# Placing the start-up work of a fused RWKV6 and tanh-shrink kernel: even loads over the first block's steps, and spaced transfers in the boot

## The chip, the cores and the metric

The kernel runs on one core of one Trainium2 chip. The metric is the time of one execution on the device in microseconds (us); medians and ranges of several executions are given. A profile is one execution, and its span (first to last instruction) is about 2 us shorter than the time. The *granted clock* is the share of full speed that TensorE's throttle allowed; 0.50 is half rate. "E", "first rest", "turn" and "block 1" below are points in a profile, in us from the start of its span.

## The reference

Four batches, eight heads, 768 tokens, 48 channels a head. A linear recurrence with decay w gives y, then a dense layer of 2048 features follows, whose activation is h - tanh(h):

```python
for t in range(S):
    cur = np.einsum('bhd,bhe->bhde', u[None] * kt, vt)
    y[:, :, t] = np.einsum('bhd,bhde->bhe', rt, state + cur)
    state = wt[:, :, :, None] * state + np.einsum('bhd,bhe->bhde', kt, vt)
...
x = y.transpose(0, 2, 1, 3).reshape(B * S, H * D)     # 3072 x 384
h = x @ w_in                                          # 384 x 2048, float64 in
out = (h - np.tanh(h)) @ w_out                        # 2048 x 384
```

## The kernel before

The 3072 tokens are cut into 8 blocks of 384. The recurrence of a block runs as *phases*: scores within chunks of 64 tokens in *levels* 1, 2, 4, 8, 16, 32 (each a batch of small products on TensorE, then decays of `kq` and `rp` and a masked copy on VectorE), a *turn* (transposes of `kq`), an *update* of the states, and a *result* that leaves x transposed in `xT`. A head of 48 channels stands in a slot of 64 rows, and `xT`, 3 x 128 rows, has six such slots. The two heads left over, called `late`, are moved into the six 16-row *holes* of the slots by six small transfers.

The dense layer of a block runs in 16 *steps*, one for each 128 features: `hp` (three products into PSUM, six matmul records), ScalarE reads it and forms squares and tanh, VectorE does five operations (the "rest"), and an accumulation `acc` follows three steps later. The phases of block i + 1 are hung between the steps of block i, so that TensorE stays full. Block 0 has no block before it: all of its phases run in a *boot*, alone. The float64 weights are loaded as pairs of words (`raw`), and *converted* by two operations on ScalarE and three on VectorE for each of 16 parts; six are converted in the boot, ten during block 0.

```python
def convert(f, raw):
    ...
    up = conv.tile([P, 2 * DM], I32, name="up", tag="up", bufs=2)
    nc.scalar.activation(out=a..., in_=hi..., func=AF.Copy, scale=HIGH_SCALE)   # w_sb
    nc.scalar.activation(out=up, in_=lo..., func=AF.Copy, scale=2.0 ** -29)
    return [shift left (VectorE), and/or with hi (VectorE), add up (VectorE)]
...
def start(self, ps):                                   # the boot
    ...
    for m in (2, 4, 8, 16, 32):
        for p0 in HALVES:
            self.level(ps, m, p0, UP)
            self.totals(m, p0, UP)
    for p0 in HALVES:
        self.turn(ps, p0)
        self.update(ps, p0)
    for p0 in HALVES:
        self.result(ps, list(range(p0, p0 + UP)), p0 != HALVES[0])
        if p0 == HALVES[0]:
            self.fill_holes([nc.sync])
...
def plan(i):                                           # which phase at which step
    names = ("level 1", 2, 4, 8, 16, 32, "turn", "update")
    first_step = 3 if i == 0 else 0
    phases = {first_step + n: name for n, name in enumerate(names)}
    result = first_step + len(names) + 1
    ...
    if i == 0:
        put(0, 1, "kmix", "rmix"); put(1, 1, "totals 1", "kq"); put(2, 1, "totals 2", "rp")
    ...                                                # later blocks: in the last six steps
...
for f in range(NF):                                    # the steps of block i
    g, next_rest = first(here, f, ps_d)
    for n, op in enumerate(rest):                      # "rest" of the step before,
        op()
        if n >= 2 and extra:                           # with a conversion woven in
            extra.pop(0)()
    ...
    if later and f in phases:
        later.phase(ps_a, phases[f])
    extra = convert(*raws.pop(0)) if raws else []      # one conversion a step from step 0
    ...
```

So in block 0 the ten conversions come one a step in steps 0 to 9, and block 1's phases come one a step from step 3 on, whatever that adds up to. In the later blocks the phases fill steps 0 to 7 and 9.

## Time and profile before

| before | |
|---|---|
| time, 3 executions | 691.12 us (689.88 to 691.14) |
| span of the profile, mean granted TensorE clock | 688.1 us, 0.984 |
| TensorE / VectorE / ScalarE busy | 94% / 82% / 69% of the span |
| last decay of the boot's levels ends on VectorE ("E") | 31.7 us |
| first `rest` starts on VectorE | 56.46 us |
| turn of block 1 starts on TensorE | 112.23 us |
| block 1's first `hp` starts | 143.94 us |
| from there to the end | 544.2 us |

The timeline of TensorE (start, duration, engine, line, operation, tile, count, and in brackets the idle time before it and who ended it), at the turn and at the start of block 1:

```profile
112.23 1.53 PE L317 MATMUL att<-ident,kq 128*128 128x128 f32 x12 [1.17 <-DVE kq L267]
...
143.94 2.10 PE L476 MATMUL hp<-xT,w_sb 128*128 128x384 f32 x6
```

A block starts at its first `hp`. The turn waits 1.17 us for a decay, a sign that VectorE sets the pace up to there. And the table of transfers between 10 and 40 us (tile, issuing queue, count, size, median us from issue to landing):

```profile
rmix<-in_rT SPq DMA_DIRECT2D x1, 768.0 KB, 8.7
```

A load for block 1, issued at 11.85 us, takes 8.7 us in a queue of others.

### The profile page before, as it was taken

Reading aid. Unit: us, or ns where it says so; the run is one execution under the profiler, and the core shown is the slowest. Engines: PE = TensorE matmul, PEld = TensorE weight load, DVE = VectorE, ACT = ScalarE, POOL = GpSimd, SP = SyncE. Lnnn points to the kernel's source line nnn. Section 1 sums busy time; section 2 is a strip of 40 time slices with the busy share of each in tenths; the row PEclk is TensorE's granted clock in tenths of the full one; section 3 lists DMA queues with packets and bytes.
Section 4 is the critical chain, followed back from the end, with each engine's and each line's share of the span. In section 5 each row is a group of like instructions: output and inputs, shape, how many; then the busy total and the mean of one; then the engine's idle time right before and its main releaser. Section 6 shows DMA issues by size and latency. Waiting matters only on the chain.

```text
span 688.1 us, 19930 instructions
## 1 busy us (share of the span) xinstructions
PE 648.3 (94%) x8480; PEld 414.8 (60%) x8480; DVE 567.4 (82%) x1139; ACT 472.5 (69%) x919; POOL 10.9 (2%) x32
## 2 busy tenths in 40 slices
PE   4766789999999999999999999999999999999997
PEld 3653455666665666666665666566665666655554
DVE  7788999999869897789879897698878898566764
ACT  3349578776768667776767667676768667788784
POOL 2010000000000000000000000000000000000000
PEclk9988899999999999999999999999999999999999
DMA  8376722241120401231130411223120010000000
GB/s 326 125 246 216 273 93 93 91 140 36 48 91 1 144 33 48 91 113 63 49 91 0 140 38 47 91 53 123 44 86 9 2 38 2 11 0 34 1 1 34
DMA packets 30840, 54.36 MB, mean 79 GB/s; under 512 B 2336, under 2 KB 28704, under 8 KB 30752
## 3 DMA queue, kind: packets, MB, share of 16 engines
q1 hardware_dynamic: 25424, 38.15, 17.1%
q0 software_dynamic: 1872, 10.22, 4.2%
q10 hardware_dynamic: 3456, 4.72, 1.8%
q8 instruction: 66, 1.08, 0.6%
q14 instruction: 22, 0.18, 0.1%
HBM read 47.19 MB, written 4.72 MB: 75 GB/s over the span
## 4 chain that ended last, share of the span: by engine, by line
PE 73%; DVE 12%; issue 5%; PEld 4%; ACT 3%; DMA 2%; SPq 1%; PEldq 1%; ACTq 0%; DVEq 0%
PE acc L514 31%; PE hp L476 29%; PE att L235 9%; DVE states L345 2%; PE att L382 2%; DVE w_sb L171 2%; PEld hp L476 2%; PE att L317 2%; PEld att L364 1%; DVE w_sb L169 1%; DVE hs L493 1%; PEld acc L514 1%; DVE rp L267 1%; DVE kq L267 1%; PE att L298 1%
## 5 line engine op out<-in xcount | busy, mean ns | idle before, releaser
L476 PE MATMUL hp<-xT,w_sb 128*128 128x384 f32 x768 | 273.1, 492 | 8.7 <-ACT h L483 5.2
L514 PE MATMUL acc<-w_sb,gT 128*128 128x384 f32 x768 | 277.7, 499 | 0.0
L476 PEld LDWEIGHTS hp<-xT,w_sb 128*128 128x128 f32 x768 | 147.0, 192 | 114.6 <-ACT h L483 8.4
L514 PEld LDWEIGHTS acc<-w_sb,gT 128*128 128x128 f32 x768 | 142.0, 192 | 90.0 <-issue 2.4
L483 ACT ACTIVATE h<-hp 128x384 f32<-128x384 f32 x128 | 62.8, 491 | 161.7 <-PE hp L476 157.9
L498 DVE TENSOR_TENSOR th<-h,th 128x384 f32<-128x384 f32 x128 | 71.1, 555 | 41.6 <-ACT th L487 41.5
L493 DVE SCALAR_TENSOR_TENSOR hs<-h,s 128x384 f32<-128x384 f32 x128 | 71.1, 556 | 21.3 <-ACT s L484 21.3
L501 DVE COPY_PREDICATED gT<-big,th 128x384 f32<-128x384 int32 x128 | 76.3, 596 | 12.9 <-ACT h L483 0.9
L485 ACT ACTIVATE qa<-s,shift 128x384 f32<-128x384 f32 x128 | 78.8, 615 | 4.2
L493 DVE SCALAR_TENSOR_TENSOR gT<-qb,hs 128x384 f32<-128x384 f32 x128 | 71.5, 558 | 9.3
L488 ACT ACTIVATE big<-s,shift 128x384 f32<-128x384 f32 x128 | 76.8, 600 | 0.0
L486 ACT ACTIVATE qb<-s,shift 128x384 f32<-128x384 f32 x128 | 76.7, 600 | 0.0
L235 PEld LDWEIGHTS att<-rp,kq 48*64 48x64 f32 x3072 | 55.0, 148 | 27.6 <-issue 16.7
L493 DVE SCALAR_TENSOR_TENSOR hs<-qa,hs 128x384 f32<-128x384 f32 x128 | 70.7, 552 | 0.0
L484 ACT ACTIVATE s<-h 128x384 f32<-128x384 f32 x128 | 67.0, 523 | 4.0
L235 PE MATMUL att<-rp,kq 48*64 48x32 f32 x3072 | 58.7, 231 | 11.5 <-DVE scores L242 4.9
L487 ACT ACTIVATE th<-h 128x384 f32<-128x384 f32 x128 | 64.9, 507 | 0.0
L267 DVE TENSOR_TENSOR kq<-kq,tot 128x768 f32<-128x768 f32 (+1 forms) x45 | 38.9, 864 | 11.5 <-PE att L235 11.5
L282 DVE COPY_PREDICATED scores<-mask_all,att 128x384 f32<-128x384 uint8 (+1 forms) x72 | 40.4, 622 | 0.0
L267 DVE TENSOR_TENSOR rp<-rp,tot 128x768 f32<-128x768 f32 (+1 forms) x45 | 38.9, 864 | 0.0
L345 DVE SCALAR_TENSOR_TENSOR states<-states,tot,att 128x48 f32<-128x48 f32 x176 | 31.6, 260 | 7.8 <-PE att L335 7.8
L235 PE MATMUL att<-rmix,kmix 48*64 48x64 f32 x768 | 14.5, 232 | 8.6 <-ACT rmix L216 7.2
(49 smaller groups left out, 343.8 us busy)
## 6 DMA issues: line engine op xcount, KB each, us to landing
raw<-in_weights POOLq DMA_DIRECT2D x13, 768.0 KB, 4.7
rmix<-in_rT SPq DMA_DIRECT2D x7, 768.0 KB, 4.6
kmix<-in_kT SPq DMA_DIRECT2D x7, 768.0 KB, 7.4
wt<-in_wT SPq DMA_DIRECT2D x7, 768.0 KB, 4.5
kq<-in_kT SPq DMA_DIRECT2D x7, 768.0 KB, 4.5
rp<-in_rT SPq DMA_DIRECT2D x7, 768.0 KB, 4.6
v_sb<-in_v SPq DMA_DIRECT2D x8, 576.0 KB, 5.8
out_y<-o ACTq DMA_DIRECT2D x24, 192.0 KB, 1.8
```

The source lines that it names most:

```text
L235: nc.tensor.matmul(dst, lhsT=lhs[rows, t0:t0 + L], rhs=src, start=True, stop=True)
L267: nc.vector.tensor_tensor(out=part, in0=part, in1=by, op=ALU.mult)
L476: nc.tensor.matmul(hp, lhsT=w_in_sb[:, f, kc, :], rhs=xT[:, kc, :], start=(kc == 0), stop=(kc == KC - 1))
L484: nc.scalar.activation(out=s, in_=h, func=AF.Square)
L485: nc.scalar.activation(out=qa, in_=s, func=AF.Square, bias=shift[:, 0:1])
L486: nc.scalar.activation(out=qb, in_=s, func=AF.Square, bias=shift[:, 1:2])
L487: nc.scalar.activation(out=th, in_=h, func=AF.Tanh)
L488: nc.scalar.activation(out=big, in_=s, func=AF.Relu, bias=shift[:, 2:3])
L493: return lambda: nc.vector.scalar_tensor_tensor(out=out, in0=in0, scalar=scalar, in1=in1, op0=op0, op1=ALU.mult)
L498: lambda: nc.vector.tensor_tensor(out=th, in0=h, in1=th, op=ALU.subtract),
L501: lambda: nc.vector.copy_predicated(out=g, mask=big.bitcast(I32), data=th)]
L514: nc.tensor.matmul(acc, lhsT=g[:, j * P:(j + 1) * P], rhs=w_out_sb[:, f, :], start=(f == 0), stop=(f == NF - 1))
```

## The change

Its intent: VectorE is the bound of block 0's middle and TensorE of everything after it, so put the ten conversions and the phases of block 1 where both engines have room (first phase in step 1 instead of 3, two conversions in step 5 and two in 11); and let TensorE's boot run without the stops it makes while bulk transfers are under way. The cut leaves out that the order on SyncE's queue is now the program's own (`manual_schedule` for PE and SP). The core of the diff, cut where "..." stands:

```diff
-RAWS = 3
+RAWS = 5                                   # buffers for unconverted weights
...
+    warm = const.tile([P, 1], F32, name="warm", tag="warm")
+    nc.scalar.activation(out=warm, in_=shift[:, 0:1], func=AF.Copy)
...
-        up = conv.tile([P, 2 * DM], I32, name="up", tag="up", bufs=2)
+        up = conv.tile([P, 2 * DM], I32, name="up", tag="up", bufs=3)
...
             for m in (2, 4, 8, 16, 32):
                 for p0 in HALVES:
-                    self.level(ps, m, p0, UP)
+                    ins = self.level(ps, m, p0, UP)
                     self.totals(m, p0, UP)
+                tc.add_manual_dep(background.pop(0)().ins, ins.ins.name, ...)   # one load behind each level
             for p0 in HALVES:
                 self.turn(ps, p0)
+            background.pop(0)()
+            for p0 in HALVES:
                 self.update(ps, p0)
...
-                    self.fill_holes([nc.sync])
+                    self.fill_holes([nc.sync, nc.scalar, nc.sync, nc.scalar, nc.sync, nc.sync])
...
-                    nc.scalar.dma_start(out=out[r0:r0 + P, :], in_=o)
+                    queue = nc.scalar if rows.stop == N else nc.sync
+                    queue.dma_start(out=out[rows, :], in_=o)
...
     def plan(i):
+        if i == 0:
+            steps = (1, 2, 3, 4, 5, 6, 8, 10, 12)          # level 1 ... 32, turn, update, result
+            before = {0: ("kmix", "rmix", "totals 1", "totals 2", "kq")}
+            behind = {1: ["rp"]}
+            converted = (0, 3, 4, 5, 5, 8, 9, 10, 11, 11)
+        else:
+            steps = (4, 5, 6, 7, 8, 9, 10, 11, 13)
+            before = {0: ("kmix",), 1: ("rmix",), 2: ("totals 1",), 3: ("totals 2", "kq"), 4: ("rp",)}
...
+        background = [ahead("rmix", rT), ahead("kmix", kT), ahead("wt", wT)]
+        background += [more_weights for _ in range(3, RAWS)] + [ahead("kq", kT)]
```

More of the change, by code (lines that the diff above doesn't have):

```diff
@@ L45 @@
 PSUM = bass.MemoryType.PSUM
-PE, DVE, ACT = (getattr(mybir.EngineType, n) for n in ("PE", "DVE", "Activation"))
+PE, DVE, ACT, SP = (getattr(mybir.EngineType, n) for n in ("PE", "DVE", "Activation", "SP"))
 B, H, S, D = 4, 8, 768, 48
@@ L156, in load_weights, with convert @@
         raw = conv.tile([P, 2 * DM, 2], I32, name="raw", tag="raw")
-        queue.dma_start(out=raw, in_=weights[f].bitcast(I32).rearrange("p (n two) -> p n two", two=2))
-        return f, raw
-    def convert(f, raw):
+        ins = queue.dma_start(out=raw, in_=weights[f].bitcast(I32).rearrange("p (n two) -> p n two", two=2))
+        return f, raw, ins
+    def convert(f, raw, _):
         lo, hi = raw[:, :, 0], raw[:, :, 1]
         a = w_sb[:, f, :].bitcast(I32)
-        up = conv.tile([P, 2 * DM], I32, name="up", tag="up", bufs=2)
+        up = conv.tile([P, 2 * DM], I32, name="up", tag="up", bufs=3)
         nc.scalar.activation(out=a.bitcast(F32), in_=hi.bitcast(F32), func=AF.Copy, scale=HIGH_SCALE)
@@ L191, in load @@
                 self.tiles[name] = inp.tile([P, NPAIR * NB], F32, name=name, tag=name)
-            nc.sync.dma_start(
+            return nc.sync.dma_start(
                 out=self.tiles[name][:, p0 * NB:(p0 + n) * NB].rearrange("d (p t) -> d p t", p=n),
@@ L266, in decay @@
                 by = t2[:, :, 1 - half].unsqueeze(2).to_broadcast([P, nblk, m])
-                nc.vector.tensor_tensor(out=part, in0=part, in1=by, op=ALU.mult)
+                ins = nc.vector.tensor_tensor(out=part, in0=part, in1=by, op=ALU.mult)
+            return ins
         def level(self, ps, m, p0, n):
@@ L271, in level @@
                 self.last_level(ps, p0, n)
-                self.decay(m, p0, n)
-                return
+                return self.decay(m, p0, n)
             gr = self.gram(ps, self.tiles["kq"], self.tiles["rp"], p0, n, m, L // 2)
-            self.decay(m, p0, n)
+            ins = self.decay(m, p0, n)
             nb = L // (2 * m)
@@ L282, in level @@
                 nc.vector.copy_predicated(out=dst, mask=mask, data=src)
+            return ins
         def last_level(self, ps, p0, n):
@@ L444, in prepare, with start @@
                 self.decay(1, 0, NPAIR, (name,))
-        def start(self, ps):
+        def start(self, ps, background):
             for p0 in HALVES:
@@ L460, in start @@
                 for p0 in HALVES:
-                    self.level(ps, m, p0, UP)
+                    ins = self.level(ps, m, p0, UP)
                     self.totals(m, p0, UP)
+                tc.add_manual_dep(background.pop(0)().ins, ins.ins.name, mybir.DependencyInfo(
+                    mybir.DependencyClass.Sync, mybir.DependencyReason.DATA))
             for p0 in HALVES:
                 self.turn(ps, p0)
+            background.pop(0)()
+            for p0 in HALVES:
                 self.update(ps, p0)
@@ L517, in add @@
                     o = dense.tile([P, DM], F32, name="o", tag="o")
+                    rows = slice(self.row0 + j * P, self.row0 + j * P + P)
                     nc.scalar.activation(out=o, in_=acc, func=AF.Copy, scale=1.0 / UPSCALE)
-                    r0 = self.row0 + j * P
-                    nc.scalar.dma_start(out=out[r0:r0 + P, :], in_=o)
+                    queue = nc.scalar if rows.stop == N else nc.sync
+                    queue.dma_start(out=out[rows, :], in_=o)
     def plan(i):
-        names = ("level 1", 2, 4, 8, 16, 32, "turn", "update")
@@ L525, in plan @@
-        first_step = 3 if i == 0 else 0
-        phases = {first_step + n: name for n, name in enumerate(names)}
-        result = first_step + len(names) + 1
-        phases[result] = "result"
-        prep = {}
-        def put(f, block, *what):
-            prep.setdefault(f, []).extend((block, name) for name in what)
-        if i == 0:
-            put(0, 1, "kmix", "rmix")
-            put(1, 1, "totals 1", "kq")
-            put(2, 1, "totals 2", "rp")
-        put(first_step + 1, i + 2, "load 1")
@@ L539, in plan @@
-        put(first_step + 7, i + 2, "load 2")
-        put(result + 1, i + 2, "load 3")
-        for f, name in zip(range(NF - 6, NF), ("kmix", "rmix", "totals 1", "totals 2", "kq", "rp")):
-            put(f, i + 2, name)
-        return phases, prep
+        names = ("level 1", 2, 4, 8, 16, 32, "turn", "update", "result")
+        if i == 0:
+            steps = (1, 2, 3, 4, 5, 6, 8, 10, 12)
[5 more added lines that the diff above has]
+            before = {0: ("kmix",), 1: ("rmix",), 2: ("totals 1",), 3: ("totals 2", "kq"), 4: ("rp",)}
+            behind, converted = {}, ()
@@ L545 @@
+        for f, name in ((steps[0] + 1, "load 1"), (steps[6] + 1, "load 2"), (steps[8] + 1, "load 3")):
+            behind.setdefault(f, []).append(name)
+        return dict(zip(steps, names)), before, behind, converted
     blocks = [Block(b, q) for b in range(B) for q in range(NQ)]
-    with tc.manual_schedule(engines={PE}), \
-            tc.tile_pool(name="ps_boot", bufs=4, space=PSUM) as boot:
+    ctx.enter_context(tc.manual_schedule(engines={PE, SP}))
+    with tc.tile_pool(name="ps_boot", bufs=4, space=PSUM) as boot:
@@ L548, with more_weights, ahead @@
         xT = blocks[0].begin()
-        start = blocks[0].start(boot)
+        raws = []
+        def more_weights():
+            raws.append(load_weights(len(raws), nc.sync))
+            return raws[-1][-1]
+        def ahead(name, src):
+            return lambda: blocks[1].load(name, src, 0, NPAIR)
+        background = [ahead("rmix", rT), ahead("kmix", kT), ahead("wt", wT)]
+        background += [more_weights for _ in range(3, RAWS)] + [ahead("kq", kT)]
+        start = blocks[0].start(boot, background)
@@ L550 @@
         next(start)
-        raws = [load_weights(0, nc.sync)]
+        more_weights()
         blocks[0].load_v()
-        for f in range(1, RAWS):
-            raws.append(load_weights(f, nc.sync))
+        for f in (1, 2):
+            more_weights()
         next(start)
@@ L559 @@
             raws.append(load_weights(f + RAWS, nc.gpsimd))
-        for name in ("load 1", "load 2"):
-            blocks[1].prepare(name)
     ps_d = ctx.enter_context(tc.tile_pool(name="ps_d", bufs=1, space=PSUM))
     ps_a = ctx.enter_context(tc.tile_pool(name="ps_a", bufs=2, space=PSUM))
-    with tc.manual_schedule(engines={PE, DVE, ACT}):
+    with tc.manual_schedule(engines={DVE, ACT}):
         blocks[1].prepare("load 3")
         waiting, rest, extra = [], [], []
+        loaded = AHEAD + RAWS
         for i, blk in enumerate(blocks):
@@ L569 @@
             later = blocks[i + 1] if i + 1 < len(blocks) else None
+            after = blocks[i + 2] if i + 2 < len(blocks) else None
             if later:
                 xT = later.begin()
-            phases, preparations = plan(i)
+            phases, before, behind, converted = plan(i)
             second = Second(blk.b * S + blk.q * NB, ps_d)
@@ L584 @@
                 rest = next_rest
-                if later and f in phases:
-                    later.phase(ps_a, phases[f])
-                extra = convert(*raws.pop(0)) if raws else []
-                for blk_p, name in preparations.get(f, ()):
-                    if blk_p < len(blocks):
-                        blocks[blk_p].prepare(name)
+                if later:
+                    for name in before.get(f, ()):
+                        later.prepare(name)
+                    if f in phases:
+                        later.phase(ps_a, phases[f])
+                    for name in behind.get(f, ()):
+                        block = after if name.startswith("load") else later
+                        if block:
+                            block.prepare(name)
+                extra = []
+                for _ in range(converted.count(f)):
+                    extra += convert(*raws.pop(0))
+                    if loaded < NF:
+                        raws.append(load_weights(loaded, nc.gpsimd))
+                        loaded += 1
                 if len(waiting) > LAG:
@@ L593 @@
                     s.add(fs, gs)
-                if i == 0 and f + AHEAD + RAWS < NF:
-                    raws.append(load_weights(f + AHEAD + RAWS, nc.gpsimd))
         for op in rest:
```

## The prediction

> **What bounds the kernel now.** I read the page's busy table, then the windows, then the waits of TensorE and VectorE, then the timeline of the first 145 us. TensorE is busy 94% of the span, so the question is where the other 6% lies. I cut the span at the starts of the first `hp` product of each block (47.46, 143.94, 222.2, ...). Columns: stretch, length, busy us of PE, PEld, DVE, ACT, POOL, then granted clock, DMA share, GB/s.
>
> ```profile
> 47.46:69.29 21.83, 16.31 (x127) 8.30 (x127) 17.36 (x29) 17.99 (x31) 2.12 (x4) 0.81 0.66 235
> 69.29:108.96 39.67, 32.45 (x542) 21.06 (x541) 39.60 (x67) 24.48 (x44) 2.65 (x5) 0.87 0.49 179
> 108.96:143.94 34.98, 33.67 (x370) 21.36 (x368) 33.88 (x76) 28.27 (x55) 0.00 (x0) 1.00 0.22 68
> ...
> 222.20:300.40 78.20, 78.06 (x1053) 49.84 (x1052) 65.86 (x131) 54.98 (x110) 0.00 (x0) 1.00 0.22 69
> ```
>
> A steady block is 78.2 us with TensorE idle 0.14 us. Block 0 is 21.83 + 39.67 + 34.98 = 96.5 us, though it has three accumulation steps fewer (they lag). Its middle is VectorE-bound: 39.60 of 39.67 us busy. So three regimes: a boot of 47.5 us, block 0 at 96.5 us, and 544 us that TensorE fills. Only the first two, and a fraction of a us at the end, can be shortened by this change.
>
> What the boot loses is in the waits (engine, who it waited for, total, times, longest) and in two windows and two timeline rows:
>
> ```profile
> PE att L235 <- issue: 3.9, 3, 2.5
> PE hp L476 <- DMA xT<-late: 3.4, 2, 3.1
> ...
> DVE w_sb L168 <- ACT w_sb L165: 4.4, 2, 4.0
> DVE kq L267 <- PE att L235: 3.0, 3, 2.4
> DVE states L345 <- PE att L335: 1.7, 2, 0.9
> ...
> 20.00:22.00 2.00, 1.06 (x31) 0.89 (x27) 2.00 (x7) 0.00 (x0) 0.00 (x0) 1.00 1.06 375
> 22.00:24.00 2.00, 0.48 (x21) 0.48 (x20) 0.48 (x2) 0.00 (x0) 0.00 (x0) 1.00 0.37 128
> ...
> 23.52 3.96 PE L235 MATMUL att<-rp,kq 48*64 48x32 f32 x127 [2.45 <-issue]
> 24.85 0.56 DVE L267 TENSOR_TENSOR kq<-kq,tot 128x384 f32<-128x384 f32 x1 [2.36 <-PE att L235]
> ```
>
> TensorE stands with nothing to wait for ("issue") until 23.52, just after the DMA share has fallen from 1.06 to 0.37; VectorE then waits 2.36 us for it. Block 1's three loads (rmix, kmix, wt, issued at 11.85 to 13.58) are what still fills the DMA then.
>
> **What the Trainium skill says.** "Runtime: NRT & Kernel Launch", section Instruction fetch mechanics: each sequencer fetches its own program by DMA, in blocks of 256 instructions, mostly hidden. The trace agrees on the block (126 and 127 pairs of load and matmul between the gaps) and not on the hiding: 2.45 us. "DMA: Bandwidth & Descriptors", section Queues, rings and completion order: an engine takes turns between its queues packet by packet; if so, a fetch should not starve, but here the gap ends with the drain, so I take the fetch as queued behind the bulk. "TensorE: Matmul & The Clock Gate", section Part 1: The HAM clock gate: after some 3.4 us idle the array runs at half rate. The trace agrees: after 3.85 us idle six `hp` records took 3.88 us against 2.10 to 2.20. "ScalarE: Activation LUTs", section What ACT_TABLE_LOAD costs: about 1283 ns; the trace has 1.28 us, at 4.68.
>
> **The change part by part.** I use start-to-start times of VectorE from the timeline, because the rows overlap: a 384-wide operation 0.47 us (0.48 for the predicated copy), a 768-wide one 0.87; so the five operations behind one `h` ("rest") 2.35, a weight conversion 0.47 + 0.87 + 0.87 = 2.2, one level's two decays 1.74 and its score copies 0.95 (1.66 for level 2, 1.81 for level 1), the 20 state updates 3.5.
>
> (1) Table load ahead of the data. It removes 1.28 us before the first scaling, but VectorE then waits for wt until 7.2 and for the second rp until 9.7 anyway. Worth 0.
>
> (2) Block 1's loads and two raws hung on the decays of levels 2, 4, 8, 16 and 32. The DMA then is clear of bulk at about 16.3 (2.36 + 3 x 0.79 + 0.59 MB at 326 GB/s), and the fetch triggered at 16.9 meets one load instead of three. I expect the waits of 2.36 and 0.19 us to go and the first 0.45 us to stay. VectorE is otherwise without a gap from 9.7 on, so the end of its levels, E, moves from 31.7 to 31.7 - 2.55 + 0.15 (two small totals come later) = 29.3.
>
> (3) Both turns before the updates. Before, TensorE did turn, update, turn, update, and the second states ended at 40.45 = E + 8.75. Now the second turn runs while ScalarE copies the first, and both states run back to back: E + 3.0 to E + 7.2. It gains 1.5 us there, of which VectorE had used 0.9 for a conversion.
>
> (4) RAWS 3 to 5, hole transfers on two queues. Before, the conversions for f = 3 to 5 waited for weights (VectorE idle 3.95 us ahead of 54.25) and the last hole landed 5.55 us after issue. Now weights 3 and 4 arrive in the boot. VectorE has 11.4 us of conversions left after the states, then kmix, rmix, totals and kq of block 1 (4.96 us): E + 7.2 + 11.4 + 4.96 = E + 23.6 = 52.9. Holes issue near E + 9.5 = 39, and even at 5.55 us the first product ends by 47.5, ahead of need at 52.9 less 4 us of ScalarE. So VectorE, not the holes, sets the start.
>
> (5) Block 0's new steps. VectorE time of steps 1 to 6, from 52.9: 7.2 (rest, conversion, level 1, rp); 5.75; 5.05; 7.25; 7.25; 8.5 (two conversions), whose last decay ends at 41.0. TensorE needs 3.5, 3.5 and 5.6 in such steps, so it follows. The turn therefore starts at 52.9 + 41.0 = 93.9. From there TensorE is the bound, for the VectorE steps are 2.35, 2.35, 4.55, 8.05, 4.55, 6.75 and stay just ahead: states end 1.2 us before `result` asks for them. From turn to block 1 the before kernel took 143.94 - 112.23 = 31.7; now there is one more dense step between them (3.87): 35.6. Block 1 starts at 129.5; I add 1.1 for cold TensorE stretches, one 0.5 us wait for ScalarE behind the two conversions of step 11, and small gaps: 130.6.
>
> (6) Block 2's preparation leaves block 0 (5.8 us of VectorE) for block 1's first steps, and so on. TensorE's work is unchanged in blocks 1 to 7, VectorE has 12 us free per block: 0. Output stores on the SyncE queue free ScalarE of two issues between the last copies: 0.4 us at the end.
>
> Sum: 143.94 - 130.6 = 13.3, plus 0.4, plus some 0.1 of small idle: 13.8 us. 691.1 - 13.8 = 677.3 us, 2.0% less.
>
> **The rivals.** A: the boot stays as long. If the fetch still meets rmix or the remaining weights, E stays near 31.7: 679.7. For it: the first gap, 1.37 us, came with no block-1 load ahead of it. Against: the drain and the restart coincide.
>
> B: VectorE is not the bound, TensorE falls cold. VectorE-paced steps leave it idle 1.4 to 1.7 us a step; in the before kernel a gap of 1.43 us was followed by an `acc` of 3.58 us instead of 2.2. If each of steps 3 to 6 loses another 1 us, block 1 starts 3 to 4 us later: 681. Against: 7.25 us a step hides most of it, and the before kernel's VectorE had no gap from 54.25 to 125.
>
> C: in the steady blocks `result` moves from step 9 to 13. It leaves about 9.7 us (two steps and one accumulation) until the next block's first product, against a median 2.5 us for a hole, 3.7 us of issuing on one queue and 0.6 us of copying, 7 us in all. If bulk gets in front of the holes, each of six boundaries could lose 1 to 3 us: 683 to 690. Against: the bulk load before it (kq, step 11) takes 4.4 us to land and is done.
>
> D: the boot gains more, because the weights no longer stall anything and the score copies are shorter than I count: 674.
>
> **Range and chances.** The central value is 677.3, range 673.5 to 682: E may be off by 1 us, the start of block 0's stream by 1, its steps by 1.5, and the rivals lean upward. The 2% line is at about 677.4 us, so faster and same are nearly even: 0.47 against 0.52, and 0.01 for slower, for which rival C would have to strike at every boundary and block 0 gain nothing.
>
> **What would show it.** In the changed profile: no "issue" gap over 1 us on TensorE between 17 and 30; the last block-0 decay at 29 to 30; both states back to back, ended by 37; no VectorE wait over 1 us for converted weights; the turn of block 1 near 94 and block 1's first `hp` near 130; later blocks at 78.2. Wrong would be: a first `hp` later than 49, VectorE with gaps in steps 1 to 6, or TensorE waiting for a hole at a block's start after 140.

## The result

The changed kernel took 681.07 us (680.40 to 681.78, 4 executions) against 690.88 us (689.88 to 691.14, 4) of the kernel before in the same rounds: a ratio of 0.9861, 95% interval 0.9844 to 0.9878, so 1.4% faster and "same" at the 2% line. A ratio, here and below, is the mean time of one kernel's runs over that of the other's in the same rounds, so not quite the ratio of the medians quoted. The time lies in the predicted range, but the gain is 9.8 us and not 13.8.

Where it came from is read from the windows of the changed kernel, cut at its own starts of `hp` (columns as in the prediction):

```profile
49.47:66.30 16.83, 12.72 (x211) 8.11 (x211) 15.98 (x27) 10.57 (x20) 1.05 (x2) 0.80 0.90 320
66.30:99.41 33.11, 31.52 (x455) 19.22 (x451) 32.68 (x52) 23.43 (x42) 2.11 (x4) 0.89 0.35 117
99.41:135.02 35.61, 35.47 (x375) 22.55 (x374) 34.68 (x77) 33.53 (x62) 0.00 (x0) 1.00 0.20 68
135.02:213.20 78.18, 78.04 (x1069) 49.78 (x1068) 67.73 (x138) 54.60 (x110) 0.00 (x0) 1.00 0.20 65
```

Block 1 starts at 135.02 instead of 143.94 us: 8.92 us. From there to the end it is 543.58 against 544.16: another 0.58. The last line is a steady block: 78.18 us against 78.20, as predicted. The third line is the tail of block 0, from its turn: 35.61 us with TensorE idle 0.14; predicted 35.6. So the missing time lies ahead of the turn, at 99.41 instead of 93.9.

The boot first. The waits of the changed kernel (over the whole execution, as in the prediction):

```profile
PE hp L486 <- DMA xT<-late: 6.8, 1, 6.8
PE att L238 <- issue: 6.0, 4, 2.6
...
DVE kq L270 <- PE att L238: 2.6, 4, 1.0
DVE w_sb L174 <- ACT up L169: 1.0, 2, 0.6
```

The second line counts a stop of 2.58 us in block 0 (at 63.58, just after a decay of VectorE that ends at 63.47). Three stops in the boot are left, 3.37 us against 3.91 before, where only the first, 1.23 us, was expected to stay. The timeline shows them at the same places in TensorE's program as before:

```profile
17.30 4.13 PE L238 MATMUL att<-rp,kq 48*64 48x32 f32 x126 [1.78 <-issue]
...
22.52 3.96 PE L238 MATMUL att<-rp,kq 48*64 48x32 f32 x127 [1.09 <-issue]
...
26.98 0.43 PE L238 MATMUL att<-rp,kq 48*64 48x32 f32 x6 [0.50 <-issue]
```

The big gap has shrunk from 2.45 to 1.09, the first has grown from 1.23 to 1.78. VectorE waits 1.00, 0.99 and 0.38 us for them, and E comes at 31.06 us instead of the predicted 29.3 (31.7 before). The spaced loads themselves do land sooner after their issue, at about half the time:

```profile
rmix<-in_rT SPq DMA_DIRECT2D x1, 768.0 KB, 4.6
```

From E to the first `rest`, in the timeline:

```profile
41.25 0.92 ACT L168 ACTIVATE w_sb<-raw 128x768 f32<-128x768 f32 x1 [2.32 <-DMA raw<-in_weights]
42.06 0.47 ACT L399 COPY late<-att 128x384 f32<-128x384 f32 x1
49.47 4.04 PE L486 MATMUL hp<-xT,w_sb 128*128 128x384 f32 x6 [6.84 <-DMA xT<-late]
55.60 0.55 DVE L503 SCALAR_TENSOR_TENSOR hs<-h,s 128x384 f32<-128x384 f32 x1
```

ScalarE stood 2.32 us for the weights of part 5, and the copy of `late`, on which the holes hang, had been put behind that conversion in its order. So the first `hp` waited 6.84 us for the holes and ran at half rate (4.04 us). The `rest` on VectorE started at 55.60: 24.5 us after E, predicted 23.6.

From the first `rest` to the turn, VectorE's bound stretch: 43.8 us, predicted 41.0. A step without a conversion between the five operations of its `rest`:

```profile
64.33 0.55 DVE L503 SCALAR_TENSOR_TENSOR hs<-qa,hs 128x384 f32<-128x384 f32 x1
64.92 0.56 DVE L503 SCALAR_TENSOR_TENSOR gT<-qb,hs 128x384 f32<-128x384 f32 x1
65.58 0.59 DVE L511 COPY_PREDICATED gT<-big,th 128x384 f32<-128x384 int32 x1
```

The second reads what the first writes, and the third overwrites parts of what the second wrote: the starts are 0.59 and 0.66 us apart, where independent neighbours start 0.47 apart. And TensorE, around level 32 of block 1:

```profile
88.93 1.01 PE L302 MATMUL att<-rp,kq 48*32 48x32 f32 x96 [1.55 <-DVE rp L270]
89.87 3.35 PE L524 MATMUL acc<-w_sb,gT 128*128 128x384 f32 x6
93.01 2.69 PE L486 MATMUL hp<-xT,w_sb 128*128 128x384 f32 x6
...
99.41 1.47 PE L321 MATMUL att<-ident,kq 128*128 128x128 f32 x12
```

After 1.55 us of waiting for VectorE the next `acc` takes 3.35 instead of 2.20 us and the `hp` 2.69 instead of 2.10: a spell at half rate. The window over it, in the changed kernel, has a granted clock (the third number from the right) of 0.50:

```profile
91.00:93.00 2.00, 2.00 (x4) 1.01 (x3) 2.00 (x5) 1.83 (x5) 0.00 (x0) 0.50 0.00 0
```

### The profile page after: what moved, and what is told of

It is laid out like the page before. It is cut to its first block, busy times and chain, and to the rows that moved or that the text cites. A ratio compares the mean times of both kernels' runs of the same rounds, so it can differ in the third digit from the quotient of the medians.

```text
span 678.6 us, 19964 instructions
## 1 busy us (share of the span) xinstructions
PE 643.7 (95%) x8480; PEld 412.9 (61%) x8480; DVE 567.3 (84%) x1139; ACT 470.2 (69%) x920; POOL 9.8 (1%) x30
## 4 chain that ended last, share of the span: by engine, by line
PE 78%; DVE 7%; issue 4%; PEld 4%; DMA 3%; ACT 3%; PEldq 0%; SPq 0%; DVEq 0%; ACTq 0%
PE acc L524 33%; PE hp L486 31%; PE att L238 9%; DVE states L349 2%; PE att L386 2%; PEld hp L486 2%; PE att L321 2%; PEld att L368 1%; DMA raw<-in_weights 1%; PE att L302 1%; DMA xT<-late 1%; PEld acc L524 1%; DMA wt<-in_wT 1%; DVE kq L270 1%; DVE hs L503 1%
```

## The experiments

**My theory** after this reading: nearly all of the gain is the placement of block 0's work (not the boot); it takes the five weight buffers to have it; the missing 4.4 us are three things in a row: program fetches that the spacing does not remove (1.8 us at E), ScalarE late with weights and `up` (0.9), and 2.8 us in VectorE's stretch, the largest single part of which is the half-rate spell. **Rivals**: the spacing or the turns carry part of the gain; the holes set the start of block 0; VectorE's share of block 1's preparation, which another engine could take, sets it; the placement is worth its gain only together with one of the small edits.

Twelve kernels ran, in four calls on one chip each; the kernel before took 690.76, 690.57, 689.97 and 690.76 us (medians of 9 to 11) beside them. All results were correct.

| run | us (range) | ratio to before, 95% | first rest | turn | block 1 | from there on |
|---|---|---|---|---|---|---|
| before | 690.88 (689.88-691.14) | 1 | 56.46 | 112.23 | 143.94 | 544.2 |
| changed | 681.07 (680.40-681.78) | 0.9861 [0.9844, 0.9878] | 55.60 | 99.41 | 135.02 | 543.6 |
| old_steps | 688.83 (687.51-690.07) | 0.9975 [0.9958, 0.9993] | 54.80 | 111.16 | 143.02 | 543.1 |
| no_spacing | 681.87 (679.28-683.51) | 0.9870 [0.9850, 0.9891] | 56.76 | 97.96 | 134.21 | 543.3 |
| turns_apart | 680.12 (679.39-680.35) | 0.9844 [0.9828, 0.9860] | 56.51 | 99.71 | 135.28 | 543.3 |
| three_raws | 685.33 (684.06-688.56) | 0.9925 [0.9904, 0.9946] | 61.84 | 105.05 | 141.00 | 543.1 |
| quiet_levels | 691.32 (690.78-692.67) | 1.0013 [0.9997, 1.0030] | 66.93 | 109.60 | 146.21 | 542.9 |
| pool_all | 681.77 (679.92-684.53) | 0.9860 [0.9843, 0.9877] | 55.16 | 100.06 | 135.68 | 546.9 |
| pool_apart | 682.69 (679.31-684.78) | 0.9883 [0.9862, 0.9905] | 54.71 | 101.14 | 137.25 | 545.9 |
| warm_32 | 680.30 (679.87-681.09) | 0.9852 [0.9837, 0.9867] | 55.87 | 97.44 | 134.71 | 543.6 |
| only_steps | 691.72 (691.54-692.90) | 1.0026 [1.0012, 1.0039] | 60.23 | 101.77 | 138.92 | 550.8 |
| small_undone | 686.05 (685.03-687.95) | 0.9941 [0.9926, 0.9957] | 54.55 | 99.25 | 135.20 | 549.8 |
| act_mix | 677.87 (677.15-679.22) | 0.9823 [0.9808, 0.9837] | 54.78 | 96.08 | 132.09 | 544.0 |
| act_mix_quiet | 676.54 (675.45-678.88) | 0.9804 [0.9784, 0.9824] | 54.06 | 95.26 | 131.37 | 543.4 |

The last column is span less block 1's start. In pool_all and pool_apart the profiled execution was one of the longer ones of its kernel; what it lost after block 1's start was not followed up.

### old_steps: the changed kernel with the placement of before

```diff
-        steps = (1, 2, 3, ...); before = ...; converted = ...
+        names = (...); first_step = 3 if i == 0 else 0     # plan() and the loop of before
+        extra = convert(*raws.pop(0)) if raws else []
```

> The changed kernel with the before kernel's placement of levels, preparations and conversions over the steps of all blocks; its boot, buffers and queues kept. Theory 1 (the placement carries the gain: in the traces, from the first 'rest' of block 0 to block 1's first product the before kernel took 143.9 - 56.5 = 87.5 us and the changed one 135.0 - 55.6 = 79.4): about 688 us, 7 us slower than the changed kernel, block 1 starting near 142, while E, the end of the boot's levels, stays at 31.1. Rival (the boot's earlier weights carry it, and the placement only follows): within 2 us of the changed kernel, about 682 to 683.

688.83 us: the whole boot part with the five buffers and the moved stores is worth 2 us, and the placement, on top of it, 7.8. Its turn is at 111.16, one us ahead of before. The first reason of the theory holds.

### no_spacing: the five background loads issued at once

```diff
+            for _ in range(5):
+                background.pop(0)()
             for m in (2, 4, 8, 16, 32):
...
-                tc.add_manual_dep(background.pop(0)().ins, ins.ins.name, ...)
```

> The changed kernel with its five background transfers issued at once instead of hung on the decays. Theory 2 (TensorE's program fetch queues behind bulk, and VectorE, which waits for it, carries the delay one for one to the turn of block 1): the 'issue' gaps of TensorE in the levels grow from 4.4 us (with the half-us one of result counted apart) to 6 to 8, E moves from 31.1 to about 33, and the time rises by about 2 us to 683. Rival (a fetch needs its 4 to 5 us whatever the DMA does, as the gap of 0.23 us in the before kernel with the DMA idle suggests): gaps as in the changed kernel, E within 0.5 us of 31.1, time within 0.5 us of 681.

The fetch gaps became 1.79, 2.46 and 0.78 us, and E came at 33.0, so the spacing does save 1.85 us there. But the time is 681.87, which cannot be told from that of the changed kernel (681.07): the intervals of the two ratios overlap. In the profile, which is of the fastest of six executions (679.28; the slowest took 683.51), the loss at E is visible at the first `rest` (56.76) and gone at the turn, which is earlier (97.96). The timeline and the window of this run at the place of the half-rate spell:

```profile
90.08 2.20 PE L524 MATMUL acc<-w_sb,gT 128*128 128x384 f32 x6
```

```profile
91.00:93.00 2.00, 2.00 (x7) 1.16 (x7) 2.00 (x4) 1.50 (x4) 0.00 (x0) 1.00 0.00 0
```

Here TensorE waited 1.56 us ahead of level 32, as long as in the changed kernel (1.55), and yet the clock stayed whole and `acc` took 2.20. The Trainium skill ("TensorE: Matmul & The Clock Gate", Part 1: The HAM clock gate) says that the window in which the gate watches activity is free-running; two equal waits at other phases with other outcomes agree with that, though nothing here shows the window itself. More profiles say the same: after a wait of 1.55 us the spell came in turns_apart and small_undone too (`acc` 3.90 and 3.31 us), and after one of 1.56 us it did not in act_mix_quiet (2.20). What follows for reading times: an edit in the boot shifts everything behind it, and may win or lose a spell by phase alone, some 1.7 us here (9.54 against 7.88 us from this `acc` to the turn) that belong to no cause in the edit. What the spacing is worth in time is therefore not shown, only that it is small.

### turns_apart: turn, update, turn, update as before

```diff
             for p0 in HALVES:
                 self.turn(ps, p0)
-            background.pop(0)()
-            for p0 in HALVES:
                 self.update(ps, p0)
+            background.pop(0)()
```

> The changed kernel with turn, update, turn, update as before. Theory 3 (VectorE's backlog sets the start of block 0's stream): VectorE waits twice for products before the states, 1.7 us in all instead of 0.6, so block 1 starts 1 us later and the time is about 682. Rival (TensorE's and the holes' path sets it): result and holes come about 0.7 us later and so does everything, which is nearly the same time, but VectorE then has a gap ahead of the first 'rest'; if neither is the bound, 681.

680.12 us: nothing lost. VectorE does wait 2.5 us for the states again. But in this order `late` was copied at 40.73, the holes were issued 1.3 us earlier, and the first `hp` started at 45.64 instead of 49.47: 3.8 us sooner. The first `rest` was still at 56.51 and the turn at 99.71. That rules out the holes as what sets the start of block 0: it is VectorE's queue of conversions and preparation, which runs here without a gap from the second states (37.76) to the first `rest`. act_mix, below, is the test from the other side.

### three_raws: three buffers for weights instead of five

```diff
-RAWS = 5
+RAWS = 3
+                if m < 16:                # only block 1's three loads are hung on levels
                     tc.add_manual_dep(...)
```

> The changed kernel with three weight buffers instead of five, so that weights 3 to 10 come through GpSimd's queue after conversions 0, 1, ... Theory 4 (the conversions ahead of block 0 wait for weights, and VectorE carries it on): VectorE waits 2 to 4 us for weights before the first 'rest', block 1 starts 2 to 4 us later, 683 to 685. Rival (holes gate the start anyway and cover it, or later slack absorbs it): within 1 us of 681.

685.33 us, 4.3 us more. The waits of VectorE in the boot say why (total, times, longest):

```profile
DVE w_sb L171 <- ACT w_sb L168: 6.8, 2, 6.5
```

Weights 3 to 5 can only be loaded when one of three buffers has been converted, and VectorE stands 6.5 us for them: first `rest` at 61.84. Five buffers are a condition of the new placement, not a gain beside it.

### quiet_levels: no bulk at all while the levels run

```diff
-        for f in (1, 2):
-            more_weights()
+        # raws 1 to 4 and rmix, kmix, wt: all hung on the last decay of level 32
```

> The changed kernel with no bulk transfer in the levels at all: only block 0's inputs, v and the first weights are loaded early, weights 1 to 4 and block 1's loads are hung on the end of level 32. It tells what of TensorE's 'issue' gaps (1.78, 1.09, 0.50 us in the changed kernel; 1.79, 2.46, 0.78 without spacing) is contention. If all of it is: gaps under 0.3 us each and E at 29.3 as predicted. If a fetch of some 127 pairs needs about 4.2 us by itself: gaps of 0.2 to 0.5 remain, the first shrinks to about 0.5, and E is 29.7. If contention plays no part: gaps and E as in the changed kernel. The time is not the point: weights come later, so VectorE waits for them after the levels; 681 to 685.

This is the test of the fetch theory. With an idle DMA one gap of 0.44 us is left in the levels, and E came at 29.1, the 29.3 of the prediction. So most of the time of the stops comes from bulk transfers. That they are program fetches can be seen in the table of transfers, asked for in windows of 0.1 us: it has packets of a kind "instruction", here one of the changed kernel (20.0:20.1) and one of the kernel before (20.9:21.0; packets, MB, share of 16 engines):

```profile
q8 instruction: 1, 0.02, 59.8%
q8 instruction: 1, 0.02, 70.5%
```

In the changed kernel they lie at 14.9, 20.0 and 24.5, and TensorE goes on at 17.30, 22.52 and 26.98; in the kernel before at 14.6, 20.9 and 24.9, and it goes on at 16.94, 23.52 and 27.71; in quiet_levels at 22.4, and it goes on at 25.00. Each stop ends 2.3 to 2.8 us after such a packet, with bulk or without. What bulk changes is how late the packet comes: 4.0 us after the products had started again with three loads under way (before, 16.94 to 20.9), 2.7 with one, rmix (changed, 17.30 to 20.0), and 1.4 with the DMA nearly idle (before, 23.52 to 24.9; DMA share 0.14).

But those transfers must come some time, and here they stood in front of the holes. Timeline of this run:

```profile
61.57 4.18 PE L487 MATMUL hp<-xT,w_sb 128*128 128x384 f32 x6 [17.37 <-DMA xT<-late]
```

First `hp` at 61.57, block 1 at 146.21, 691.32 us in all. E gained 2 us and block 1's start lost 11.2: the bulk can be moved, but not away.

### pool_all and pool_apart: block 1's preparation on GpSimd

```diff
-            before = {0: ("kmix", "rmix", "totals 1", "totals 2", "kq")}
+            before = {0: ('kq',)}
...
         next(start)
+        for name in ('rmix', 'kmix', 'totals 1', 'totals 2'):
+            blocks[1].prepare(name, nc.gpsimd)
```

pool_apart has the same edit and that of turns_apart.

> The changed kernel with kmix, rmix and all totals of block 1 made by GpSimd during the boot, so VectorE has 4.1 us less to do ahead of block 0's first 'rest'. If VectorE alone set the start (the prediction's reading): first 'rest' at 51.5, time 677. If the holes of xT stand close behind VectorE (in the changed kernel the first product ends at 53.5, its square at 54.6, and the 'rest' starts at 55.6): the first 'rest' moves by only about 1 us, to 54.6, and the time by at most 1 us, 680.

> The kernel with turns apart (whose holes happened to land 4 us earlier: first product at 45.6 instead of 49.5, with no gain) and the same work moved to GpSimd. If VectorE and the holes are the two limits one behind the other, removing both must pay what neither paid alone: first 'rest' at 52 to 52.5, time 676.5 to 677.5. If something else sets block 0 (TensorE's half-rate spells, ScalarE): 680.

Both missed. They free VectorE of some 4 us of work (the prediction counted 4.96 us for it together with `kq`, which is 0.87 and stays), and no time was won: 681.77 against 681.07 of the changed kernel, and 682.69 against 680.12 of turns_apart. In the timeline of pool_all, a GpSimd operation and its neighbours on VectorE:

```profile
29.86 1.47 POOL L256 TENSOR_TENSOR tot<-wt 128x768 f32<-128x768 f32 x1 [2.94 <-DMA wt<-in_wT]
29.94 1.43 DVE L256 TENSOR_TENSOR tot<-tot 128x24 f32<-128x24 f32 x1
...
31.76 1.18 DVE L270 TENSOR_TENSOR rp<-rp,tot 128x384 f32<-128x384 f32 x1
```

The small total on VectorE takes 0.17 us elsewhere in the same run, and here 1.43: it ends with GpSimd's operation (both at 31.3 to 31.4). The decay takes 1.18 instead of 0.54. The skill ("SBUF — State Buffer", section SBUF: two separate sides) says that a VectorE operation with two SBUF inputs and a GpSimd operation that reads SBUF exclude each other for the whole instruction; this trace agrees. E slipped to 34.4 (31.06 in the changed kernel), which ate what the shorter list of work had saved: the first `rest` came only 0.4 us sooner. GpSimd is no free engine next to VectorE.

### warm_32: two idle products ahead of block 1's level 32

```diff
+            if filler is not None:           # block 0 only; the result is overwritten
+                for _ in range(2):
+                    nc.tensor.matmul(ps_t[:, 0, 0:NB], lhsT=w_in_sb[:, 0, 0, :], rhs=filler[:, 0, :],
+                                     start=True, stop=True)
```

> The changed kernel with two filler matmuls (128x384, result overwritten) in TensorE's idle 1.55 us ahead of block 1's level 32. In the changed kernel the acc and hp after that idle took 3.35 and 2.69 us instead of 2.2 and 2.1, while without spacing they took 2.20 and 2.10 and block 1 started 0.8 us earlier although its levels ended 1.85 us later. If the half-rate spell is on the path to block 1 and follows from the idle time: acc and hp at 2.2 and 2.1, turn at 97.5, block 1 at 133.2, time 679.3. If the spell falls by the phase of a free-running window and not by this gap: the same 681, or the spell moves elsewhere.

The spell is gone (`acc` 2.20, `hp` 2.10; the wait ahead of level 32 is down from 1.55 to 0.17 us) and the turn comes at 97.44 instead of 99.41: 2.0 us won there. That the two products removed it is not shown by this one profile, for no_spacing and act_mix_quiet are without the spell at the full wait. The time is 680.30, only 0.8 less than the changed kernel, for block 1 starts at 134.71. The rest went further on, in the result:

```profile
120.82 0.31 PE L390 MATMUL att<-scores,v_sb 64*48 64x64 f32 x2 [1.12 <-issue]
```

A stop of 1.12 us with nothing to wait for, inside the result's products. It is a program fetch again: an "instruction" packet lies at 118.1, 2.7 us before the stop ends, with the DMA otherwise idle. In the changed kernel these products run in one piece. And the result now starts on the heels of VectorE's states (116.12, the states ending at 116.27), so that its first 96 products take 1.92 us instead of 1.63. Together 1.4 us, most of what was won.

### only_steps: the kernel before with the new placement alone

```diff
 # before: plan() and the loop of the changed kernel; RAWS = 3, boot, stores as before
```

> The before kernel with the new placement over the steps of all blocks, and nothing else of the change. With old_steps (boot changes alone: 688.8) it completes a square: before 691, both 681. If the two halves add up: 691 - (691 - 681.1) + (691 - 688.8) = 683.3. If the new steps need the earlier weights, as three_raws (685.3, VectorE waiting 6.5 us for weights) suggests: 685 to 687, with that wait in the trace.

691.72 us, a little slower than before. Its block 1 starts 5.0 us earlier (138.92), and would probably be earlier still but for a wait of 3.37 us for weights, as in three_raws (first `rest` at 60.23), but the rest of the span is 550.8 instead of 544.2: a loss of 6.6 us in the steady blocks, which nothing in the prediction has. Each against the kernel before in its own rounds, by the ratios: the boot edits alone (old_steps) win 1.7 us, the placement alone loses 1.8, both together win 9.6. The two parts are plainly not additive.

### small_undone: the small edits taken back

```diff
-    nc.scalar.activation(out=warm, ...)                       # table load
-    self.fill_holes([nc.sync, nc.scalar, nc.sync, nc.scalar, nc.sync, nc.sync])
+    self.fill_holes([nc.sync])
-    queue = nc.scalar if rows.stop == N else nc.sync
+    queue = nc.scalar                                         # stores of the output
```

> The changed kernel without its small parts: no early table load, holes all on SyncE's queue, every output store on ScalarE's. Table and holes are worth nothing if VectorE sets the start (first 'rest' still at 55.6), the stores 0.3 to 0.4 us at the end: 681.0 to 681.5 against 681.1. If the two queues for the holes mattered: 682 to 683 with the first product after 51.

Block 1 starts at 135.20, so the table load and the two queues for the holes are worth nothing there. But the time is 686.05: 5 us lost, all after block 1's start (549.8 against 543.6). It is the same loss as in only_steps, and the timeline of this run at a boundary of two blocks shows the cause:

```profile
227.26 0.47 ACT L527 ACTIVATE o<-acc 128x384 f32<-128x384 f32 x1
227.75 0.34 ACTq L529 DMA_DIRECT2D out_y<-o  x1
227.90 2.71 PE L522 MATMUL acc<-w_sb,gT 128*128 128x384 f32 x6
228.19 0.49 ACT L527 ACTIVATE o<-acc 128x384 f32<-128x384 f32 x1 [0.47 <-PE hp L484]
```

Each copy of a finished accumulator is followed by the issue of its store on the same engine, so the copies start 0.93 to 0.97 us apart. The accumulators have one buffer each: the next block's first `acc` follows at 227.90 and waits for the copies (2.71 instead of 2.20 us and what came before it). In the changed kernel the three copies are one group:

```profile
147.92 1.23 ACT L529 ACTIVATE o<-acc 128x384 f32<-128x384 f32 x3
```

Three in 1.23 us, 0.4 apart. Who waited for the tile `o` (total us, times), in small_undone and then in the changed kernel:

```profile
  PEld acc L522: 11.3, 21
```

```profile
  PEld acc L524: 2.3, 7
```

The kernel before had its stores on ScalarE too, and lost nothing by it: there, a level of the next block stands in step 3, ahead of that `acc`, and gives the copies 1.6 us. The new placement begins the levels in step 4 and takes this cover away; moving the stores to SyncE pays for it. The last column of the table has all four cases: old placement 544.2 (stores on ScalarE) and 543.1 (SyncE, old_steps), new placement 549.8 (ScalarE) and 543.6 (SyncE). The prediction had put the stores down as 0.4 us at the very end.

### act_mix: ScalarE scales block 1's kmix and rmix in the boot

```diff
+        def mix_ahead(self, name):
+            t = self.tiles[name].rearrange("d (p n two) -> d p n two", p=NPAIR, two=2)
+            for p in range(NPAIR):
+                half = t[:, p, :, 1 if name == "kmix" else 0]
+                nc.scalar.activation(out=half, in_=half, func=AF.Copy, scale=u_sb[:, p:p + 1])
...
-            before = {0: ("kmix", "rmix", "totals 1", "totals 2", "kq")}
+            before = {0: ("totals 1", "totals 2", "kq")}
...
         next(start)
+        for name in ("rmix", "kmix"):
+            blocks[1].mix_ahead(name)
```

with the edit of turns_apart.

> A candidate: turns apart, and kmix and rmix of block 1 scaled by ScalarE in the boot, where it stands idle 7.8 us ahead of level 32, instead of by VectorE (two operations of 0.87 us). GpSimd slowed VectorE down in pool_all (a decay of 0.54 us took 1.2 to 1.8); ScalarE should not. If VectorE's work up to block 1's states is the bound: first 'rest' 1.7 us earlier than with turns apart alone (56.5), 54.8, block 1 near 133.5, time 679. If a half-rate spell or a program fetch of TensorE takes its place: no change, 680 to 681.

677.87 us, 3.2 less than the changed kernel. As the edit of turns_apart is in it, the share of ScalarE is read against that run: 2.2 us by the medians (680.12), 1.4 by the ratios. It takes 1.74 us of work (two operations of 0.87) from VectorE, which sets the pace, and VectorE's decays beside it keep their 0.55 us. The first `rest` is at 54.78 instead of 56.51, 1.73 us earlier, as it must be if VectorE's queue sets it. The stretch to the turn is 41.3 us, for the half-rate spell does not occur. Whether by phase or because TensorE now waits less there (1.37 us), this run cannot tell; in act_mix_quiet it does not occur at 1.56 us either.

### act_mix_quiet: the same, and another order of the loads

```diff
-        background = [ahead("rmix", rT), ahead("kmix", kT), ahead("wt", wT)] + [raw 3, raw 4] + [kq]
+        background = [raw 1, raw 2] + [ahead("rmix", rT), ahead("kmix", kT), ahead("wt", wT)] + [raw 3, raw 4] + [kq]
-                tc.add_manual_dep(...)                        # one a level
+                for _ in range(2 if m in (2, 32) else 1): tc.add_manual_dep(...)
```

> act_mix (677.9) with weights 1 and 2 also taken out of the stretch of TensorE's first program fetch: they are hung on level 2, block 1's loads on levels 4, 8 and 16, weights 3 and 4 on level 32. If bulk ahead of a fetch makes it late (quiet_levels: one gap of 0.44 us, E 29.1): the first gap, 1.78 us, shrinks under 0.6, E comes 1 us earlier than in act_mix (31.0), and, if VectorE's backlog still sets block 0, block 1 starts at 131.2 instead of 132.1 and the time is 677. Against: the scaling on ScalarE now stands between the two copies of the turned keys and may hold the second update up by 1 us, which gives it back: 678.

676.54 us. The first two fetch gaps are gone; the third grew, in the timeline of this run:

```profile
26.49 0.43 PE L238 MATMUL att<-rp,kq 48*64 48x32 f32 x6 [1.81 <-issue]
```

E comes at 30.6, 0.4 us ahead of act_mix. The gap moved to another fetch. This is the fastest kernel of the study by its median, 2.0% below before ("unclear" at the 2% line) and 4.5 us below the change as given; its interval overlaps that of act_mix, so that the new order of loads is worth something is not shown.

## Why the prediction was right or wrong

The time was within the range, whose upper end (682) the rivals had raised, and the class was the likelier one by 0.52 to 0.47; the gain was 9.8 instead of 13.8 us. By its steps:

1. *Table load, worth 0.* Block 1's start in small_undone agrees (135.20 against 135.02), though the hole queues were undone with it.
2. *Spacing ends two of the three fetch waits; E at 29.3.* Mechanism right (quiet_levels: E at 29.1 without bulk; no_spacing: 33.0 with all of it), size wrong. VectorE waited 1.00, 0.99 and 0.38 us where 0.45, 0 and 0 stood: E was 31.06, +1.8 us. The second fetch met one load (rmix, issued at 16.16) and was still 1.09 us late. The first, which had none of block 1's loads ahead of it and was expected to stay as it was, met weights 1 and 2: it is gone where they are moved (act_mix_quiet). Rival A, "the fetch still meets rmix or the remaining weights", was what happened. And the sign named for it, an "issue" gap over 1 us between 17 and 30, was there.
3. *Turns ahead of updates.* States back to back and ended by 37.8, as predicted to within 0.8; worth nothing in time (turns_apart).
4. *VectorE and not the holes sets the start, at 52.9.* The mechanism held: turns_apart had the first `hp` 3.8 us earlier and no earlier `rest`. But the term E + 23.6 was E + 24.5: 0.57 and 0.44 us of waiting for `up` from ScalarE, which stood for the weights of part 5. The sum had no term for ScalarE. The holes were misjudged (issued at E + 11.5, not E + 9.5, and the first `hp` 6.9 us after that), which did no harm: the prediction's alarm, "a first `hp` later than 49", went off at 49.47 and meant nothing.
5. *41.0 us to the turn, then 35.6.* The second was 35.61. The first was 43.81. In it the five slots from `rest` to `rest` took 7.80, 6.41, 5.38, 7.22 and 7.24 us, where 7.2, 5.75, 5.05, 7.25 and 7.25 stood: +1.5. A `rest` with no conversion between its operations is 2.68 us and not 2.35, because dependent operations start 0.59 and 0.66 apart (I had taken 0.47 for all), and there were waits of 0.32 and 0.25 us. The sixth slot, 8.5 predicted, lasted 9.76 up to the turn: +1.3, and that is rival B. In the changed kernel TensorE needs 9.54 us from the `acc` at 89.87 to the turn; in no_spacing, with a whole clock, 97.96 - 90.08 = 7.88. Rival B had been sized at 1 us in each of four steps; it struck once where it counted.
6. *Steady blocks 0, stores 0.4 us at the end.* The net was right (0.58 us) by luck: two errors cancelled. The new placement costs each steady block about 0.9 us at its step 3, unless the stores are off ScalarE; the store edit is worth some 6 us of span (549.8 against 543.6), not 0.4 (under the old placement 1.1: 544.2 against 543.1). Rival C, holes at the block boundaries, did not happen.

The missing time adds up: 1.8 (E) + 0.9 (`up`) + 2.8 (slots and spell) - 1.1 (the allowance that had been added for just such things) = 4.4 us, and block 1's start is 135.02 - 130.6 = 4.4 us late. Left open: what holds the packet of a program fetch back while bulk is under way, and why it takes another 2.3 to 2.8 us to the next product; and why the spell after level 32 comes in some runs and not in others at equal waits, beyond its agreeing with a free-running window.

## What to carry to other kernels

When a change moves the start of work, ask what it had been covering: here a level in step 3 hid ScalarE's stores, and only a second edit, booked as a trifle, kept 6 us from being lost. Relieve the engine that sets the pace by giving work to one that does not slow it down in turn: against turns_apart, ScalarE won 1.4 to 2.2 us (act_mix) where GpSimd lost 2.6 (pool_apart). And count dependent neighbours on VectorE at their own spacing, not at that of independent ones.

## What the Trainium skill lacked or had wrong

- "Runtime: NRT & Kernel Launch", Instruction fetch mechanics, has the crossing of a block mostly hidden. On TensorE in streams of small products it was not: gaps of 1.1 to 2.5 us under bulk transfers (changed: 1.78 and 1.09; no_spacing: 2.46), and 0.44 and 1.12 us with an idle DMA (quiet_levels, warm_32). That fetches lengthen with bulk is not on the page.
- "DMA: Bandwidth & Descriptors", Queues, rings and completion order: has an engine take turns between queues packet by packet, from which one expects a fetch to pass bulk almost freely. Its packet came 4.0 us after the products had started again with three loads under way, 2.7 with one and 1.4 with a nearly idle DMA (quiet_levels, above).
- "TensorE: Matmul & The Clock Gate", Part 1: The HAM clock gate, gives an idle window of some 3.4 us as what lowers the clock. Here 1.55 us without a product (88.93) was followed by a granted clock of 0.50, and 1.56 us in another run was not. The page also has a case where frequent short idles were enough; how little activity in a window lowers the clock is not stated there.
- "DMA: Bandwidth & Descriptors" has sequencer cycles for a transfer's instruction only in a section on a newer chip; no page that I read says what an issue costs between two operations of the engine that issues it: copies on ScalarE started 0.93 to 0.97 us apart with a store between, and 0.4 without.
- No page that I read gives the spacing of dependent VectorE operations in a row: 0.59 and 0.66 us at 128x384 in fp32, against 0.47 for independent ones.
